# Attention with RMS-normed queries and keys, then a SwiGLU block: copies of the transposed keys on ScalarE, left sums of the output one third of a group sooner, loads of values and stores of results given out later

## The chip, the cores and the metric

The kernel runs on one core of a Trainium2 chip. The metric is the device time of one launch in microseconds (us), as the median of the runs. PE is TensorE (matrix products; PEld is its loading of weights), DVE is VectorE, ACT is ScalarE, POOL is GpSimd, and SP is SyncE, which here does nothing but issue DMAs.

## The reference

There are 8 batches of 12 heads with 448 positions of 64 elements. What is computed, in NumPy and cut to the essentials:

```python
def rmsnorm(x, g):
    return x / np.sqrt(np.mean(x * x, axis=-1, keepdims=True) + 1e-06) * g
q_n, k_n = rmsnorm(q, g_q), rmsnorm(k, g_k)
attn = softmax(q_n @ k_n.transpose(0, 1, 3, 2) / 8)
x = (attn @ v).transpose(0, 2, 1, 3).reshape(8 * 448, 768)
xn = rmsnorm(x, rms_g)
g = xn @ w_gate                                # 768 -> 1536
y = (g * sigmoid(g) * (xn @ w_val)) @ w_out    # 1536 -> 768
```

All data are float32. The rows of attention's output (3584 x 768) are the tokens of the second part.

## The kernel before

**Attention.** Each batch b has six groups of two heads, 48 groups g in all. For a group, queries and keys are loaded (`load_pair`), their squares summed (L493 on ACT, L496 on DVE), the inverse norms made on POOL (L515), keys scaled on ACT (L530) and queries on POOL (L520). `turn(g, i)` transposes: for i = 0 three transposes of queries (L544) and one of the last rows of queries and keys (L548), for i = 1 three of the keys. From the time that there is work of the second part, both use a PSUM pool of one buffer, so a transposition waits until the one before it has been copied out:

```python
    nc.scalar.activation(st["qT", g], ps[:, 0:S], ACT.Copy, scale=gqk[:, 0:1])   # L549
    nc.vector.tensor_copy(st["kT", g][:, LAST], ps[:, S:])                       # L550, 128x64
else:
    nc.vector.tensor_copy(st["kT", g][:, FULL], ps[:, FULL])                     # L552, 128x384
```

Scores (L658), exponentials on ACT (L663) and products with the values (L673) follow step by step; the sums of the exponentials are made on POOL (L708, L713, L643). The values of group g + 2 are loaded by `load_v`, two DMAs (L432) on SP, within the steps of group g.

**The second part.** When a batch's six groups are through, its tokens are normed (L725, L727, L729, L743) and their products with gate and value weights made, each as a scheme of block products with sums of the blocks on both sides: sums of the tokens (L771 on DVE), products on PE (L1177), evictions from PSUM by DVE (L1195, L1198) or ACT (L1192), and SwiGLU (L1205, L1209, L1210). The first batch's is done by plain products (L1581). The weights for it are prepared early on (integer operations, L963 on POOL, and sums of blocks, L1082 and L1085 on DVE), stored to DRAM and loaded again in blocks of 192 or 256 KB (`ask`, L1061). The sums of the blocks of output weights come from `derive_o` (L1117 on DVE), each stored by SP (L951) two steps later, and those for the second scheme of the output from `derive_q` (L1145 to L1148, stores L1152 and L1155). Side loads, of the blocks that these two need (L1043), go into places of one kind, "side". In `arena`, a memory of equal units, "side", "wg" and the others are spans of units.

**The output.** A batch's output follows while the next batch is in attention. `out_strassen` (L1442 on PE) does it with seven products of blocks. `out_quads`, used for five of the batches, nests a second scheme in each of the seven, i = 0 to 6, whose left operands are again sums (`left_q1`, L1387, three of S1 to S3 and one S4). Its products (L1513) are done in thirds, in this order on PE:

```python
for i in range(len(ORDER_Q) + 1):
    if i < len(ORDER_Q):
        steps.append((full, lambda i=i: a(i)))
    if i:
        steps.append((full // 2, lambda i=i - 1: d(i)))
    if i < len(ORDER_Q):
        steps += [(full, lambda i=i: bb(i)), (full, lambda i=i: c(i))]
```

`a`, `bb` and `c` each make two products in one PSUM bank; `d` makes one more on top of half of c's bank. On the way out DVE adds: L1533 (after ACT's copy L1532) behind a, L1538 and L1539 and the sum S4 behind bb, L1545 behind c, and then S1 to S3 of the next i; at i = 1 also those that are left of the sums of the outer scheme for the second half (`hurry(first_sums)`, L1359). L1556 follows d, then sums on POOL (L1484), and stores by SP (L1339) two steps later.

**What sets the order.** The program writes the order out by hand. `pe(fn)` advances a count of steps, gives out the instructions of fn, and then what `after(n, ...)` has put off until this step; every engine and the queue of SP work through their instructions in the order in which they were given out. Between the steps of attention, `fill` takes items of the second part from a list `todo`, as many as their share of the time allows, and after each gives out at most one sum of tokens or of left operands, and later in the group calls `derive`, `derive_o` (three times less the operations that `derive` made) and `derive_q`.

Of the kernel before, what the change touches and what calls it, by code (L numbers as in the profile page):

```python
# [12 lines left out]
ALU = mybir.AluOpType  # L13
# [322 lines left out]
def safe_scores(  # L336
# [195 lines left out]
    def turn(g, i):  # L532


        if g >= NG:
            return
        b, hp = divmod(g, NPAIR)
        if ("qT", g) not in st:
            for part in ("qT", "kT"):
                st[part, g] = qkT_pool.tile([128, S], F32, name=part)  # L540
        src = st.pop(("qn", g)) if i == 0 else st["qk", g][:, 1]
        ps = (ps_m if todo else ps_f).tile([128, 512], F32, name="tr", tag="m" if todo else "f")
        for t in range(NK):
            nc.tensor.transpose(ps[:, t * 128:(t + 1) * 128], src[:, t * 2 * D:(t + 1) * 2 * D], ident)  # L544
        if i == 0:
            if g == 0:
                warm(5)
            nc.tensor.transpose(ps[:, NK * 128:], st["rest", b][:, hp].rearrange("p h d -> p (h d)"), ident)  # L548
            nc.scalar.activation(st["qT", g], ps[:, 0:S], ACT.Copy, scale=gqk[:, 0:1])  # L549
            nc.vector.tensor_copy(st["kT", g][:, LAST], ps[:, S:])  # L550
        else:
            nc.vector.tensor_copy(st["kT", g][:, FULL], ps[:, FULL])  # L552

    def score(g, cs):

# [328 lines left out]
        after(3 if key[0:2] == ("wg", 1) else 1, free)  # L884

    def data(key):
        return st[key][0]

    def load_raw(src):
        raw = raw_pool.tile([128, 2 * BW], I32, name="raw")  # L890
# [144 lines left out]
    def ask():  # L1035

        if turn_of["n"] < TURNS:
            return
        while side and room(1, "side"):
            key = side.pop(0)  # L1040
            asked[key] = now["t"]
            st[key] = block("side")
            nc.sync.dma_start(out=data(key), in_=home(key))  # L1043
        while asked["n"] < len(uses):
            key = uses[asked["n"]]
            kind, keep_free = "wg" if key[0] == "wg" else "w", 3
            if key[1] == 1 and key[0] == "wg":
                kind, keep_free = "wg1", 6
            elif asked["derived"] < len(derived):
                return  # L1050
            if key[0] == "wo" and key[2][0] == "T" and ("kept", *key[2:]) not in asked:
                return
            if key[0] == "wq" and asked.get("sums_q", 0) < KG * (key[2] + 1):
                return
            if not room(keep_free + 1, kind):
                return
            asked["n"] += 1
            asked[key] = now["t"]
            st[key] = block(kind)
            src = home(key)  # L1060
            nc.sync.dma_start(out=data(key)[:, 0:src.shape[-1]], in_=src)  # L1061
# [68 lines left out]
    def derive_q(wait=5):  # L1130

        if not todo_q or sums_o or now["t"] - asked.get("at_q", 0) < 3 or not room(2, "wg"):
            return False
        i, j = todo_q[0]
        keys = [("wx", 2, ORDER_Q[i], c) for c in (j, j + KG)]
        for key in keys:
            if asked.get(key, now["t"]) > now["t"] - wait:
                return False
        todo_q.pop(0)
        own_a, own_b = ("ta", i, j), ("tb", i, j)  # L1140
        st[own_a], st[own_b] = block("wg"), block("wg")
        asked["at_q"] = now["t"]
        x, y, ta, tb = (data(key)[:, 0:BW].rearrange("p (h n) -> p h n", h=2) for key in (*keys, own_a, own_b))

        nc.vector.tensor_tensor(tb[:, 1], x[:, 1], x[:, 0], ALU.subtract)  # L1145
        nc.vector.tensor_tensor(ta[:, 1], y[:, 1], x[:, 1], ALU.subtract)
        nc.vector.tensor_tensor(ta[:, 0], y[:, 1], tb[:, 1], ALU.subtract)
        nc.vector.tensor_tensor(tb[:, 0], y[:, 0], ta[:, 0], ALU.subtract)  # L1148

        def store():  # L1150
            parts = kept_q[i].rearrange("p (n w) -> p n w", w=HW)
            nc.sync.dma_start(out=parts[:, j], in_=x[:, 0])  # L1152
            for src, first, second in ((y, 1, 6), (ta, 2, 3), (tb, 4, 5)):
                gap = (second - first) * KG
                nc.sync.dma_start(out=parts[:, first * KG + j:second * KG + j + 1:gap], in_=src)  # L1155
            asked["sums_q"] = asked.get("sums_q", 0) + 1

        after(1, store)
        for key in (*keys, own_a, own_b):
            after(3, lambda key=key: used(key))  # L1160
        return True
# [229 lines left out]
    def out_strassen(b):  # L1391
# [17 lines left out]
        def final(ps, pair, n, i, other=None):  # L1409
            y = y_pool.tile([128, HALF], F32, name="y", tag="y")  # L1410
            if other is None:
                nc.scalar.copy(y, ps)
            else:
                nc.vector.tensor_tensor(y, ps, add[other, pair], ALU.add)
            after(1, lambda: store(b, n, i, y))

        def done(name, pair):
            ps = bank[name, pair]
# [38 lines left out]
    def out_quads(b):  # L1457
# [19 lines left out]

        def out(what, n, first):
            for row in range(2):
                after(2, lambda row=row: store(b, n, tiles[first + row], what[row]))  # L1480

        def add(to, one, other):
            for row in range(2):
# [51 lines left out]
        def bb(i):  # L1535
# [2 lines left out]
            nc.vector.tensor_tensor(u[:, 0], ps[:, 0], st.pop(("q1", b, i)), ALU.add)  # L1538
            nc.vector.tensor_tensor(u[:, 1], ps[:, 1], u[:, 0], ALU.add)  # L1539
            left_q1(b, i, (3,))  # L1540

        def c(i):
            ps = two(i, "c")
            u3 = st["u", b, i][:, 1:2].to_broadcast([128, 2, HW])
            nc.vector.tensor_tensor(dst[i][1].rearrange("p (h n) -> p h n", h=2), ps, u3, ALU.add)  # L1545
            if i == 1:
                hurry(first_sums)
            if i + 1 < len(ORDER_Q):
                left_q1(b, i + 1, range(3))
            if i + 2 == len(ORDER_Q):  # L1550
                st["l2 done", b] = True

        def d(i):
            ps = bank[i, "c"]
# [67 lines left out]
    def fill(n=None):  # L1622

        if n is None:
            part["slot"] += 1
            upto = part["all"] * min(part["slot"] / part["slots"], 1.0)
            n = 0
            while n < len(todo) and part["spent"] + todo[n][0] / 2 < upto:
                part["spent"] += todo[n][0]
                n += 1  # L1630
        for _ in range(min(n, len(todo))):
            _, turns, sums_made, fn = todo.pop(0)
            while turn_of["n"] < turns:
                if not convert():
                    pe(idle)
            made, key = sums_made or (0, None)
            while asked["derived"] < made or (key and key not in st):
                before = dict(asked)
                derive(0)
                if key and key[0] == "wo":  # L1640
                    derive_o(0)
                ask()
                if before == asked:
                    pe(idle)
            pe(fn)
            convert()

            if first_sums:
                first_sums.pop(0)()
            elif slow and now["t"] - st["block"] > 4 and now["t"] - st["x_at"] >= NPAIR and may_make(slow[0][0]):  # L1650
                slow.pop(0)[1]()
            if 2 < now["t"] - st["block"] < 5:
                derive()
            if now["t"] - st["block"] > 4 and now["t"] != st.get("left_sums"):
                made = 0
                while made < 2:
                    done = derive()
                    if not done:
                        break
                    made += done  # L1660
                for _ in range(3 - made):
                    derive_o()
                derive_q()

# [99 lines left out]
    for g in range(NG + 1):  # L1764
# [51 lines left out]
        if g == NPAIR + 1:  # L1816
            some = lambda *parts: [exps(g, i, scores(g, i)) for i in parts]
            pe(lambda: (rests(g), some(0, 1)))
            pe(lambda: rms_x(0))
            pe(lambda: values(g - 1))  # L1820
            load_v(g + 2)
            pe(lambda: some(2, 3))
            pe(lambda: norm_x(0))
            pe(lambda: some(4, 5))
            pe(lambda: sums(g - 1))
            later_sums(g, 2)
            begin(0, 15)
        else:
            sums_due = g % 2 == 0
            pe(lambda: (totals(g - 1) if sums_due else None, step(g, 0)))  # L1830
            pe(lambda: [step(g, i) for i in (1, 2)])
            load_v(g + 2)
            pe(lambda: [step(g, i) for i in (3, 4)])
            pe(lambda: ([step(g, i) for i in (5, 6)], weigh(g - 1, 2) if sums_due else hold(g - 1)))
            if g < NG:
                later_sums(g, 2)
        st["block"] = now["t"]
        if hp:
            fill()
            norm_k(g + 1, 0)  # L1840
# [21 lines left out]
        pe(lambda: norm_x(b - 1))  # L1862
        fill()
    fill(len(todo))
    for _ in range(3):
        pe(idle)


# [36 lines left out]
```

## Time and profile before

| what | value |
|---|---|
| time, median of 3 runs | 1554.34 us (1552.52 to 1556.89) |
| time of the profiled execution | 1555.48 us |
| its span, first to last instruction | 1553.7 us |
| mean clock granted to TensorE | 0.990 |
| busy share of PE, DVE, ACT, POOL | 96%, 68%, 37%, 47% |
| DMA, mean | 208 GB/s |

The span is from the first to the last instruction of one execution, and busy times are shares of it. A row "A <- B" in the waits tells how long engine and line A stood idle until B was done; in a timeline the same stands in brackets behind the instruction, and "x3" behind an instruction is a run of three of the same kind. PEclk is the granted clock as a share of full speed. The line numbers are those of the kernel before.

### The profile page before, as it was taken

What the parts mean: (1) busy time and instruction counts of PE and PEld (TensorE: products, weight loads), DVE (VectorE), ACT (ScalarE), POOL (GpSimd) and SP (SyncE); (2) the same over time, 40 slices, a digit from 0 to 9 for tenths busy, and PEclk for the clock granted to TensorE, in tenths of its full rate; (3) what the DMA queues carried; (4) which work ended last, traced back from release to release, by engine and by line L of the source; (5) the groups of instructions that cost most, each with busy time, mean ns of one, the idle gap of its engine ahead of it and who ended that gap; (6) DMA issues with size and microseconds to landing.
All of it is one profiled execution on the core that took longest, in us unless ns stands there. A gap on an engine that the chain in (4) does not pass through costs nothing. (4 is left out here: it accounts for less than half of the span.)

```text
span 1553.7 us, 25676 instructions
## 1 busy us (share of the span) xinstructions
PE 1493.5 (96%) x8732; PEld 1163.8 (75%) x8732; DVE 1051.9 (68%) x1906; ACT 582.2 (37%) x1297; POOL 732.1 (47%) x708
## 2 busy tenths in 40 slices
PE   8999998988899999999999999999999999999997
PEld 4344444676765778888888889858788889899997
DVE  5787987688875577884668745644668745685664
ACT  6856664334322343323432253334442342201110
POOL 6867986546433353365534635435544633021002
PEclk9999999999999999999999999999999999999999
DMA  7758585666576999977456765566456664488566
GB/s 191 229 153 237 173 245 157 195 211 199 182 242 209 294 305 314 295 229 242 138 167 188 229 225 174 159 212 200 127 160 199 219 203 148 147 266 264 172 209 196
DMA packets 302176, 322.51 MB, mean 208 GB/s; under 512 B 81620, under 2 KB 243668, under 8 KB 302036
## 3 DMA queue, kind: packets, MB, share of 16 engines
q1 hardware_dynamic: 301108, 320.58, 66.5%
q8 instruction: 72, 1.18, 0.3%
q14 instruction: 68, 0.56, 0.1%
q10 hardware_dynamic: 800, 0.20, 0.1%
q0 software_dynamic: 128, 0.00, 0.0%
HBM read 266.90 MB, written 53.77 MB: 206 GB/s over the span
## 5 line engine op out<-in xcount | busy, mean ns | idle before, releaser
L1177 PE MATMUL ff<-x,w 128*128 128x224 f32 x1272 | 259.9, 359 | 0.9 <-DVE pb L1198 0.5
L713 POOL TENSOR_TENSOR es<-es,e 128x448 f32<-128x448 f32 x205 | 251.2, 1225 | 13.6
L1177 PEld LDWEIGHTS ff<-x,w 128*128 128x128 f32 x1272 | 243.5, 194 | 5.0 <-issue 1.4
L658 PE MATMUL sc<-qT,kT 64*64 64x448 f32 x1176 | 231.7, 539 | 2.3 <-DVE kT L552 2.1
L673 PE MATMUL av<-e,vt 64*64 64x448 f32 x984 | 193.2, 538 | 0.0
L663 ACT ACTIVATE e<-sc 128x448 f32<-128x448 f32 x294 | 155.3, 546 | 85.5 <-PE sc L658 69.1
L1177 PE MATMUL ff<-xs,w 128*128 128x224 f32 x848 | 168.9, 353 | 6.6 <-DMA w<-kept 4.9
L1177 PEld LDWEIGHTS ff<-xs,w 128*128 128x128 f32 x848 | 158.5, 190 | 10.8 <-issue 8.6
L643 POOL TENSOR_TENSOR ss<-ss,rd 128x448 f32<-128x448 f32 x40 | 46.7, 1169 | 209.3 <-ACT rd L642 208.0
L708 POOL TENSOR_TENSOR es<-e 128x448 f32<-128x448 f32 x41 | 47.2, 1152 | 201.9 <-ACT e L663 201.9
L658 PEld LDWEIGHTS sc<-qT,kT 64*64 64x64 f32 x1176 | 79.0, 133 | 83.3 <-issue 57.2
L1513 PE MATMUL ff<-w,l 128*128 128x192 f32 x630 | 118.6, 329 | 6.0 <-DVE l L1387 3.7
L1198 DVE TENSOR_TENSOR pc<-ff,l 128x448 f32<-128x448 f32 x56 | 34.9, 623 | 122.3 <-PE ff L1177 75.3
L515 POOL TENSOR_TENSOR rs<-ms,mhalf 128x12 f32<-128x12 f32 (+1 forms) x50 | 114.8, 2295 | 4.2
L1581 PE MATMUL ff<-x,w 128*128 128x448 f32 x288 | 114.5, 552 | 0.0
L1513 PEld LDWEIGHTS ff<-w,l 128*128 128x128 f32 x630 | 103.6, 190 | 12.1 <-DVE l L1387 5.2
L673 PEld LDWEIGHTS av<-e,vt 64*64 64x64 f32 x984 | 66.5, 133 | 41.4 <-issue 41.4
L1195 DVE TENSOR_TENSOR pb<-ff,pb 128x448 f32<-128x448 f32 x84 | 52.3, 623 | 66.2 <-PE ff L1177 58.8
L1581 PEld LDWEIGHTS ff<-x,w 128*128 128x128 f32 x288 | 54.5, 194 | 52.6 <-issue 50.6
L1177 PE MATMUL ff<-top_x,w 128*128 128x224 f32 x424 | 88.0, 357 | 2.4 <-ACT pa L1192 1.2
L1177 PEld LDWEIGHTS ff<-top_x,w 128*128 128x128 f32 x424 | 78.6, 190 | 14.2 <-issue 10.5
L1177 PE MATMUL ff<-l,w 128*128 128x224 f32 x432 | 86.8, 353 | 0.7 <-DVE pc L1198 0.7
(208 smaller groups left out, 2803.9 us busy)
## 6 DMA issues: line engine op xcount, KB each, us to landing
w<-kept SPq DMA_DIRECT2D x383, 256.0 KB, 3.7
w<-kept_q SPq DMA_DIRECT2D x350, 192.0 KB, 3.7
w<-kept_o SPq DMA_DIRECT2D x150, 192.0 KB, 3.7
kept_q<-w SPq DMA_DIRECT2D x63, 192.0 KB, 3.8
qk<-in_q_dram SPq DMA_DIRECT2D x48, 192.0 KB, 3.7
qk<-in_k_dram SPq DMA_DIRECT2D x96, 96.0 KB, 3.7
raw<-in_moe_w_gate_dram SPq DMA_DIRECT2D x24, 384.0 KB, 4.5
raw<-in_moe_w_val_dram SPq DMA_DIRECT2D x24, 384.0 KB, 3.9
```

Source lines behind the costliest of these rows:

```text
L515: nc.gpsimd.tensor_tensor(st["rs", g][:, cols], ms, mhalf[:, cols], ALU.pow)
L643: after(m, lambda: (nc.gpsimd.tensor_tensor(ss, ss, rd, ALU.add), st.update({("summed", b): hp})))
L658: nc.tensor.matmul(ps[r, 0:S], lhsT=st["kT", g][r, keys_of(i)], rhs=st["qT", g][r, :], start=True, stop=True)
L663: nc.scalar.activation(e, ps[:, 0:S], ACT.Exp)
L673: nc.tensor.matmul(st["av", g][own(j), 0:S], lhsT=vt, rhs=st["e", g, i][r], start=i == 0, stop=i == PARTS - 1, skip_group_check=True)
L708: nc.gpsimd.tensor_tensor(st["es", g], st["e", g, 0], st["e", g, 1], ALU.add)
L713: nc.gpsimd.tensor_tensor(st["es", g], st["es", g], st["e", g, i], ALU.add)
L1177: nc.tensor.matmul(bank[:, w * HT:(w + 1) * HT], lhsT=data(key)[:, (2 * w + c) * 128:(2 * w + c + 1) * 128], rhs=a[left][:, c, :], start=o ...
L1195: nc.vector.tensor_tensor(T[name], ps[:, 0:S], T[name], ALU.add)
L1198: nc.vector.tensor_tensor(T[name], ps[:, 0:S], T[other], what)
L1513: nc.tensor.matmul(ps, lhsT=a[:, j, :], rhs=data(key)[:, n % 2 * HW:(n % 2 + 1) * HW], start=start and j == 0, stop=j == KG - 1, skip_grou ...
L1581: nc.tensor.matmul(bank[w][:, 0:S], lhsT=data(key)[:, c * 128:(c + 1) * 128], rhs=st["x", 0][:, 3 * half + c, :], start=half == c == 0, st ...
```

## The change

The copies of the transposed keys are made by ScalarE in place of VectorE in those groups in which work of the second part is in the list; the first groups keep VectorE. Side loads of blocks of output weights may also take a place of the kind "wg", once more than 32 sums of gate and value weights have been derived; `data` cuts the block to its kind's width. The results' stores are given out two steps instead of one after their last operation in `out_strassen`, and four instead of two in `out_quads`. There, the left-over sums at i = 1 and S1 to S3 of the next i are given out at the end of bb(i) instead of the end of c(i), so they stand ahead of L1545 on VectorE. `derive_o` is not called in a step in which `derive` made something, and otherwise two times, three from the 33rd derived sum on. The values of group g + 2 are loaded two steps after the last of the group's own steps, not among them, and five steps instead of three without work end the program.

```diff
--- before.py
+++ after.py
@@ -539,6 +539,7 @@
             for part in ("qT", "kT"):
                 st[part, g] = qkT_pool.tile([128, S], F32, name=part)
         src = st.pop(("qn", g)) if i == 0 else st["qk", g][:, 1]
+        copy_k = nc.scalar.copy if todo else nc.vector.tensor_copy
         ps = (ps_m if todo else ps_f).tile([128, 512], F32, name="tr", tag="m" if todo else "f")
         for t in range(NK):
             nc.tensor.transpose(ps[:, t * 128:(t + 1) * 128], src[:, t * 2 * D:(t + 1) * 2 * D], ident)
@@ -547,9 +548,9 @@
                 warm(5)
             nc.tensor.transpose(ps[:, NK * 128:], st["rest", b][:, hp].rearrange("p h d -> p (h d)"), ident)
             nc.scalar.activation(st["qT", g], ps[:, 0:S], ACT.Copy, scale=gqk[:, 0:1])
-            nc.vector.tensor_copy(st["kT", g][:, LAST], ps[:, S:])
+            copy_k(st["kT", g][:, LAST], ps[:, S:])
         else:
-            nc.vector.tensor_copy(st["kT", g][:, FULL], ps[:, FULL])
+            copy_k(st["kT", g][:, FULL], ps[:, FULL])
 
     def score(g, cs):
 
@@ -884,7 +885,7 @@
         after(3 if key[0:2] == ("wg", 1) else 1, free)
 
     def data(key):
-        return st[key][0]
+        return st[key][0][:, 0:GW if key[0] == "wg" else BW]
 
     def load_raw(src):
         raw = raw_pool.tile([128, 2 * BW], I32, name="raw")
@@ -1036,10 +1037,10 @@
 
         if turn_of["n"] < TURNS:
             return
-        while side and room(1, "side"):
+        while side and (room(1, "side") or side[0][0] == "wd" and asked["derived"] > 32 and room(4, "wg")):
             key = side.pop(0)
             asked[key] = now["t"]
-            st[key] = block("side")
+            st[key] = block("side" if room(1, "side") else "wg")
             nc.sync.dma_start(out=data(key), in_=home(key))
         while asked["n"] < len(uses):
             key = uses[asked["n"]]
@@ -1140,7 +1141,7 @@
         own_a, own_b = ("ta", i, j), ("tb", i, j)
         st[own_a], st[own_b] = block("wg"), block("wg")
         asked["at_q"] = now["t"]
-        x, y, ta, tb = (data(key)[:, 0:BW].rearrange("p (h n) -> p h n", h=2) for key in (*keys, own_a, own_b))
+        x, y, ta, tb = (data(key).rearrange("p (h n) -> p h n", h=2) for key in (*keys, own_a, own_b))
 
         nc.vector.tensor_tensor(tb[:, 1], x[:, 1], x[:, 0], ALU.subtract)
         nc.vector.tensor_tensor(ta[:, 1], y[:, 1], x[:, 1], ALU.subtract)
@@ -1412,7 +1413,7 @@
                 nc.scalar.copy(y, ps)
             else:
                 nc.vector.tensor_tensor(y, ps, add[other, pair], ALU.add)
-            after(1, lambda: store(b, n, i, y))
+            after(2, lambda: store(b, n, i, y))
 
         def done(name, pair):
             ps = bank[name, pair]
@@ -1477,7 +1478,7 @@
 
         def out(what, n, first):
             for row in range(2):
-                after(2, lambda row=row: store(b, n, tiles[first + row], what[row]))
+                after(4, lambda row=row: store(b, n, tiles[first + row], what[row]))
 
         def add(to, one, other):
             for row in range(2):
@@ -1538,17 +1539,17 @@
             nc.vector.tensor_tensor(u[:, 0], ps[:, 0], st.pop(("q1", b, i)), ALU.add)
             nc.vector.tensor_tensor(u[:, 1], ps[:, 1], u[:, 0], ALU.add)
             left_q1(b, i, (3,))
-
-        def c(i):
-            ps = two(i, "c")
-            u3 = st["u", b, i][:, 1:2].to_broadcast([128, 2, HW])
-            nc.vector.tensor_tensor(dst[i][1].rearrange("p (h n) -> p h n", h=2), ps, u3, ALU.add)
             if i == 1:
                 hurry(first_sums)
             if i + 1 < len(ORDER_Q):
                 left_q1(b, i + 1, range(3))
             if i + 2 == len(ORDER_Q):
                 st["l2 done", b] = True
+
+        def c(i):
+            ps = two(i, "c")
+            u3 = st["u", b, i][:, 1:2].to_broadcast([128, 2, HW])
+            nc.vector.tensor_tensor(dst[i][1].rearrange("p (h n) -> p h n", h=2), ps, u3, ALU.add)
 
         def d(i):
             ps = bank[i, "c"]
@@ -1658,7 +1659,7 @@
                     if not done:
                         break
                     made += done
-                for _ in range(3 - made):
+                for _ in range(0 if made else 3 if asked["derived"] > 32 else 2):
                     derive_o()
                 derive_q()
 
@@ -1818,7 +1819,6 @@
             pe(lambda: (rests(g), some(0, 1)))
             pe(lambda: rms_x(0))
             pe(lambda: values(g - 1))
-            load_v(g + 2)
             pe(lambda: some(2, 3))
             pe(lambda: norm_x(0))
             pe(lambda: some(4, 5))
@@ -1829,12 +1829,12 @@
             sums_due = g % 2 == 0
             pe(lambda: (totals(g - 1) if sums_due else None, step(g, 0)))
             pe(lambda: [step(g, i) for i in (1, 2)])
-            load_v(g + 2)
             pe(lambda: [step(g, i) for i in (3, 4)])
             pe(lambda: ([step(g, i) for i in (5, 6)], weigh(g - 1, 2) if sums_due else hold(g - 1)))
             if g < NG:
                 later_sums(g, 2)
         st["block"] = now["t"]
+        after(2, lambda g=g: load_v(g + 2))
         if hp:
             fill()
             norm_k(g + 1, 0)
@@ -1862,7 +1862,7 @@
         pe(lambda: norm_x(b - 1))
         fill()
     fill(len(todo))
-    for _ in range(3):
+    for _ in range(5):
         pe(idle)
 
 
```

## Prediction

> **What bounds the kernel.** I read the page first, then the waits of PE, then a table of windows around PE's long waits, then timelines at two places. In the page the busy times are shares of the 1553.7 us span, and the slices of PEclk are tenths of full clock.
>
> ```profile
> PE 1493.5 (96%) x8732; PEld 1163.8 (75%) x8732; DVE 1051.9 (68%) x1906; ACT 582.2 (37%) x1297; POOL 732.1 (47%) x708
> PEclk9999999999999999999999999999999999999999
> ```
>
> PE carries the time. Nothing in the diff removes a matmul, so only PE's idle time (some 50 us in the trace) and stretches at a lower clock can change. The waits of PE (total, times, longest) say what ends that idle time:
>
> ```profile
> PE tr L544 <- DVE kT L550: 14.2, 5, 5.1
> PE ff L1177 <- DMA w<-kept: 4.9, 3, 3.5
> PE ff L1513 <- DVE l L1387: 3.7, 5, 1.2
> PE ff L1177 <- DVE pc L1198: 3.7, 3, 2.5
> PE sc L658 <- DVE kT L552: 2.1, 1, 2.1
> PE ff L1513 <- DVE pc L1545: 1.5, 3, 0.5
> ```
>
> The first row is the largest: the one buffer for transposes is freed only when DVE has copied the keys. Its five waits end at 240.05 (5.10 us), 428.48 (3.47), 627.51 (2.68), 814.79 (1.48) and 1163.77 (1.49), each at the boundary of two batches. Windows around two of them, and around the 3.53-us wait for weights at 510.87 (columns: length, PE, PEld, DVE, ACT, POOL busy, PEclk, DMA share, GB/s):
>
> ```profile
> 236.00:239.30 3.30, 0.00 (x0) 0.00 (x0) 3.23 (x5) 0.00 (x0) 2.96 (x3) 1.00 0.73 179
> 239.31:246.12 6.81, 6.07 (x11) 3.21 (x12) 6.60 (x16) 0.00 (x0) 4.22 (x4) 0.50 0.71 176
> 816.17:819.57 3.40, 3.40 (x11) 3.08 (x10) 1.30 (x3) 0.58 (x1) 2.80 (x3) 0.50 0.29 81
> 507.00:514.00 7.00, 3.47 (x26) 2.10 (x28) 2.19 (x6) 1.50 (x3) 0.00 (x0) 1.00 1.01 343
> ```
>
> After each of the five waits PE runs 3.4 or 6.8 us at clock 0.50; after the wait at 510.87 it does not. PE work in such a stretch takes twice its time (a matmul of L1177 every 374 ns, not 189), so half the PE busy time in it is lost: 3.04 and 2.69 us in the two long ones (at 239 and 427), 1.7 in each short one, 10.8 in all. Why DVE is late is seen at 811 to 815 (start, duration, instruction):
>
> ```profile
> 811.13 0.63 ACT L549 ACTIVATE qT<-tr,gqk 128x448 f32<-128x448 f32 x1 [5.94 <-PE tr L548]
> 811.82 1.37 DVE L1387 TENSOR_TENSOR l<-l,h 128x384 f32<-128x384 f32 x1
> 813.12 1.48 DVE L1387 TENSOR_TENSOR h<-h 128x384 f32<-128x384 f32 x1
> 814.52 0.21 DVE L550 COPY kT<-tr 128x64 f32<-128x64 f32 x1
> 814.79 0.55 PE L544 MATMUL tr<-ident,qk 128*128 128x128 f32 x3 [1.48 <-DVE kT L550]
> ```
>
> ACT was done with its half of the buffer at 811.76; the 0.21-us copy stands behind DVE's sums.
>
> **Key copies on ScalarE.** From group 8 on, 40 of 48 pairs of L550 and L552 (0.22 and 0.55 us) leave DVE: 31 us. On ACT their price is estimated from its own PSUM copies, 0.53 (L1192, 128x448) and 0.32 (L1532, 128x192): 0.48 and 0.21, 28 us on an engine 37% busy. What stands behind them there are exponentials and gate copies; the bounds are 0 and +0.7 us at each of 80 places (not below: ACT gains no time), and I take 0, since ACT is idle before most of its groups. L550's copy follows L549 at once (811.8 above), so PE no longer waits. At 240 the whole 5.10+3.04 = 8.1 goes: DVE and ACT are idle later, and the next weights lead their use by 38 us. At 627, 815, 1164: 2.68+1.7 = 4.4, 1.48+1.7 = 3.2, 1.49+1.7 = 3.2; next in line is L1195's eviction, in each case 0.5 us or more early. The single L552 wait at 188.86 adds 2.1. At 428 the 3.47+2.69 does not stand, see the next part. Sum: -21.0.
>
> Here a rule bears on it. The Trainium skill (TensorE: Matmul & The Clock Gate, Part 1: The HAM clock gate) has the clock halved only after an idle window of about 3.4 us on a free-running grid. By it the three dips after waits of 1.48 to 2.68 us would have another cause and remain (5.1 us less gained), and no new wait below 3.4 us would cause one; the sum at the end would be 1551 instead of 1547.5. The rows above, where all five waits dip, are what I sum by.
>
> **Fewer derived sums per step (L1117), side loads into a second kind of space.** Before, each late step called derive_o at least once; after, not at all where derive made something, else two or three times. In 300 to 312 DVE is always behind: four L1117 (0.55 to 0.86) stand ahead of the eviction L1198 that PE waits for (2.46 at 312.77, 0.48 at 315.04). Without them, 2.94 falls to about 0.3: 2.6. The waits at 360 to 375 (5.05) shrink by an estimated 0.9, that at 397.56 by 0.65; one at 404.96 grows by 0.5. Sum -3.65. The deferred L1117 come later: the last stands at about 438.8, the eight stores of kept_o wait for it on SP, and a load of wo behind them lands (3.7 us) at 443.0 while PE wants it at 441.15. With DVE three L1117 behind at 428 this eats the gain of that boundary; bounds -6.2 (the whole gain) to +4, taken +1.9.
>
> **Loads of values and stores later.** v loads (two DMAs, L432) are given out two steps after the group's scores instead of among them, stores two steps (out_quads) or one step (out_strassen) later. SP stands idle before L432 for 59.3 and 51.5 us (for PE) and before L1339 for 31.3 (for POOL), and loads of weights queue behind both. PE pays for late weights only in the second row of its waits, 4.9 us. At 510.87 the load goes out some 2 us sooner: 1.8 of 3.53 won (bounds 0 and 4.9; below nothing by 1.2, if the bunched kept_q stores get ahead of it). In the quads the loads of kept_q lead by 3 us or more, so deferring buys nothing there. The two more idle steps at the end issue nothing to PE: 0. Sum -1.8.
>
> **Left sums one third sooner.** In out_quads, for the batches output at 636-702, 823-890, 1172-1236, 1353-1402 and 1494-1544, PE does thirds a, (d of the one before), bb, c: two products of 0.98 us in each, one in d, 7.0 in a cycle. d(i) writes the bank that L1545 reads, and needs it 4.0 us after bb(i) ends. Before, L1545 came ahead of S1, S2, S3 (L1387) of the next i. Now they stand ahead of it. Nothing is added, only the order on DVE. Alone, the chain is .1 + .72 (L1538, L1539) + 4 x .47 + .55 (L1545), some 3.4: it fits. Two places do not. At i = 1 the three remaining hurried sums (L1359) also go ahead, back to back from 655.1 to 656.5 in the trace of before: L1545 ends 657.75 for a d at 656.36, +1.5. At i = 5 POOL contends:
>
> ```profile
> 688.73 1.29 DVE L1387 TENSOR_TENSOR l<-raw,l 128x384 f32<-128x384 f32 x1
> 689.55 5.48 POOL L713 TENSOR_TENSOR es<-es,e 128x448 f32<-128x448 f32 x4
> 691.00 0.55 DVE L1545 TENSOR_TENSOR pa<-ff,th 128x384 f32<-128x384 f32 x1
> 693.97 1.48 DVE L1387 TENSOR_TENSOR raw<-raw 128x384 f32<-128x384 f32 x1
> 694.11 1.24 PE L1513 MATMUL ff<-w,l 128*128 128x192 f32 x6 [0.76 <-DVE l L1387]
> ```
>
> The sums take 1.18 to 1.48 beside L713. From 690.0 three of them (4.0) and two L496 (1.0) put the end of L1545 at 695.6, for a d at 692.2: +3.4, less the waits of 0.92 that S1 to S3 cost PE before: +2.5. At i = 2, by the same reckoning, +1.25 if POOL stays beside it, 0 if not; i = 3 gives back 0.4. I take +0.4 for the two. That is 4.4 in each of the first three batches; the fourth, where 1.3 of waits go, +1.5; the last +1.2. Sum +15.9 (bounds: 19.4 with all contended rows, and -5.2 if nothing is late and the waits for L1387 and L1545 go). One of the three new waits of 3.4 us is taken to dip the clock (as five of nine waits above 1.4 us did), +1.7.
>
> **Sum.** -21.0 - 3.65 - 1.8 + 1.9 + 15.9 + 1.7 = -6.9. The profiled execution took 1555.48 us (span and 1.8 around it), 1.1 above the median of the runs: 1548.5 there, 1547.5 as a median. What a measurement of this kernel can tell from no change is 0.3%, 4.7 us.
>
> **Rivals.**
> - *The sums never make L1545 late except at i = 1.* For it: uncontended sums are .55, and the mean of L1387 over its groups is .62 to .86, so most stand clear of POOL; DVE also loses the 31 us of copies. Against it: POOL's L713 follows the same steps as before. Then i = 5 and i = 2 cost nothing and their waits go: 15.9 + 1.7 becomes about 2, and the time is 1532 (1529 to 1541).
> - *Slower: L1545 behind the left sums brings the clock dips back.* Every new wait above 1.2 us in the quads (three in each of three batches, two and one in the others: 12) halves the clock for 3.4 us, at 1.7 each: 20.4, and with the contended 19.4 the loss is 39.8 against 24.6 won elsewhere: +15, 1569 (1559 to 1573). It decides from six dips on with contended sums, or eight with mine. For it: a wait of 1.48 was enough at 815. Against it: those five stood beside the eight one-column matmuls of L725, and 3.53 us at 510.87 did not dip.
> - *The waits only change their name.* At the boundaries PE meets the next late item (L1195, L727, weights) as at 428, and the total stays within 4.7 us. Against it: DVE has idle time after 240 and 815.
>
> **How the numbers follow.** My sum, own range 1543 to 1553: 0.45, of which 0.11 lies within 4.7 us of before. First rival 0.20, slower rival 0.30, renamed waits 0.05. Faster .34 + .20 = 0.54, same .11 + .05 = 0.16, slower 0.30. The range leaves out a tenth at each end: half of the first rival below 1533, a third of the slower one above 1566.
>
> **What would show it.** Right: no row of L544 waiting for a key copy, clock 1.00 after 240, 627, 815 and 1164, no wait of L1177 for L1198 above 0.5; rows of L1513 waiting for L1545's line of together 15 to 22 us, longest 3 to 4, at i = 1 and i = 5. Wrong: L1513's waits below 8 us (first rival), or windows of clock 0.50 inside the quads (slower rival), or L1442 waiting over 4 us for kept_o near 441 (the deferred sums), or ACT named as the releaser of PE at the boundaries.

## The result: 0.7% slower

The changed kernel took 1564.89 us (median of 6 runs, 1563.31 to 1568.73) against 1554.01 for the kernel before (6 runs). The ratio is 1.0072, with a 95% interval of 1.0054 to 1.0090. Forecast was 1547.5, faster; the time lies inside the stated range (1533 to 1566), on the other side of the kernel before. The profiled execution, the fastest of the six, has a span of 1561.5 us, 7.8 more than before.

The page of the changed kernel has PE, DVE and ACT as follows:

```profile
PE 1491.8 (96%) x8732; PEld 1160.1 (74%) x8732; DVE 1027.2 (66%) x1826; ACT 603.8 (39%) x1377; POOL 734.1 (47%) x708
```

Eighty copies have gone from DVE to ACT: 24.7 us less on DVE, 21.6 more on ACT (the copies alone took 27.1 there; forecast 31 and 28). The busy time of PE is 1.7 us less, so the loss is idle time. In the waits of PE (line numbers are one higher than before from L545 on, and L1545 is now L1552) the names have changed:

```profile
PE ff L1514 <- DVE pa L1552: 11.2, 4, 3.3
PE ff L1514 <- DVE y L1552: 8.7, 7, 2.3
PE sc L659 <- DVE x L744: 5.5, 1, 5.5
PE ff L1178 <- DMA w<-kept: 5.4, 2, 4.2
PE ff L1514 <- DVE pb L1552: 4.5, 3, 1.5
PE ff L1178 <- DVE pb L1196: 3.6, 3, 3.0
PE ff L1178 <- DVE w L1086: 2.8, 1, 2.8
PE sc L659 <- ACT rd L699: 1.5, 1, 1.5
```

The first row of before, 14.2 us for the keys' copy, is gone. The waits for the eviction behind the left sums are now 24.4 us together (three rows), and there is a new wait for L744, where before there was none. Below, the quads are the five stretches in which `out_quads` runs, and a dip is a stretch at a granted clock of 0.50.

Since the order on PE is the same in both programs, the start of the same matmul can be compared in the two traces. The table has, at some times of the trace before, by how much the changed kernel is ahead (-) or behind (+), and the same for three kernels of the experiments:

| us in the trace before | 200 | 270 | 412 | 444 | 608 | 640 | 709 | 826 | 895 | 1090 | 1173 | 1240 | last matmul |
|---|---|---|---|---|---|---|---|---|---|---|---|---|---|
| changed | -2.2 | -1.3 | -3.1 | -2.8 | -0.1 | -4.2 | 1.3 | -2.1 | 3.1 | 1.9 | -1.6 | 5.5 | 9.1 |
| u_sums | -3.8 | -3.8 | -3.8 | -1.9 | 3.1 | -1.0 | -2.7 | -6.0 | -6.5 | -7.8 | -11.3 | -11.7 | -11.7 |
| k_only | -3.9 | -3.5 | -4.4 | -5.5 | -3.2 | -0.1 | 0.2 | -3.1 | -3.6 | -4.9 | -8.4 | -8.8 | -8.8 |
| x744 | -4.1 | -10.9 | -10.8 | -10.4 | -5.9 | -9.9 | -11.7 | -15.0 | -15.5 | -16.8 | -20.2 | -20.7 | -20.7 |

Up to 636 us the changed kernel and u_sums have the same program. Of their 2.5 us at 270, 1.6 come from the first 10 us, where no part of the change is at work yet (k_only and x744 have the same lead); the 3 us at 608 are what two executions of one program differ by. A third kernel that is the same up to there, late_i1 below, is at +6.3 at 608.

### The profile page after: what moved, and what is told of

Read it like the earlier page. It is cut to its first block, busy times and chain, and to the rows that moved or that the text cites. A ratio compares the mean times of both kernels' runs of the same rounds, so it can differ in the third digit from the quotient of the medians.

```text
span 1561.5 us, 25665 instructions
## 1 busy us (share of the span) xinstructions
PE 1491.8 (96%) x8732; PEld 1160.1 (74%) x8732; DVE 1027.2 (66%) x1826; ACT 603.8 (39%) x1377; POOL 734.1 (47%) x708
## 4 chain that ended last, share of the span: by engine, by line
PE 79%; DVE 14%; DMA 3%; issue 2%; SPq 1%; ACT 1%; POOL 0%; DVEq 0%; POOLq 0%; ACTq 0%
PE ff L1178 35%; PE ff L1514 12%; PE sc L659 7%; PE av L674 7%; PE ff L1443 5%; PE ff L1582 5%; PE tr L545 2%; PE ff L1316 2%; DVE l L1388 1%; PE den L692 1%; PE den L607 1%; PE sc L563 1%; PE av L590 1%; DVE w L1118 1%; DVE ms L496 1%
## 5 line engine op out<-in xcount | busy, mean ns | idle before, releaser
L714 POOL TENSOR_TENSOR es<-es,e 128x448 f32<-128x448 f32 x205 | 251.0, 1224 | 13.6
L1178 PE MATMUL ff<-x,w 128*128 128x224 f32 x1272 | 254.0, 353 | 1.4 <-DVE pb L1199 1.1
L1178 PEld LDWEIGHTS ff<-x,w 128*128 128x128 f32 x1272 | 238.6, 190 | 4.2 <-DVE pb L1199 1.4
L1196 DVE TENSOR_TENSOR pb<-ff,pb 128x448 f32<-128x448 f32 x84 | 52.3, 623 | 65.3 <-PE ff L1178 55.9
L1582 PEld LDWEIGHTS ff<-x,w 128*128 128x128 f32 x288 | 53.3, 190 | 51.0 <-issue 47.6
L1178 PEld LDWEIGHTS ff<-top_x,w 128*128 128x128 f32 x424 | 78.8, 190 | 13.9 <-issue 13.7
```

Of the source, the lines that this page charges most:

```text
L714: nc.gpsimd.tensor_tensor(st["es", g], st["es", g], st["e", g, i], ALU.add)
L1178: nc.tensor.matmul(bank[:, w * HT:(w + 1) * HT], lhsT=data(key)[:, (2 * w + c) * 128:(2 * w + c + 1) * 128], rhs=a[left][:, c, :], start=o ...
L1196: nc.vector.tensor_tensor(T[name], ps[:, 0:S], T[name], ALU.add)
L1582: nc.tensor.matmul(bank[w][:, 0:S], lhsT=data(key)[:, c * 128:(c + 1) * 128], rhs=st["x", 0][:, 3 * half + c, :], start=half == c == 0, st ...
```

## Experiments

**1. The left sums behind the eviction again (u_sums).** All else is as changed.

```diff
 def bb(i): ...
-    if i == 1: hurry(first_sums)
-    if i + 1 < len(ORDER_Q): left_q1(b, i + 1, range(3))
 def c(i): ...   # ends with the eviction
+    if i == 1: hurry(first_sums)
+    if i + 1 < len(ORDER_Q): left_q1(b, i + 1, range(3))
```

> The changed kernel with the left sums back behind L1545's eviction (all else changed). Theory 1: the order of these sums is the whole loss. The trace of the changed kernel has 24.4 us of waits of PE for that eviction and two clock dips of 3.4 us (1.7 us each) inside the quads, the kernel before had 5.2 us of waits there: about 20.9 us less, 1544 us (1541 to 1547), under the kernel before. Rival: VectorE is late in the quads anyway and the sums are waited for by name of L1388 instead: 1555 us or more.

Measured: 1541.94 us, ratio to before 0.9905 (0.9884 to 0.9927), as expected. Of the waits of PE for DVE in the quads this row is left, with 0.5 us more for other sums of L1388 and 0.7 for L1546:

```profile
PE ff L1514 <- DVE l L1388: 3.7, 5, 1.2
```

So the order of the sums costs 23.0 us by the medians, and 24.0 by the table from 640 us on (13.3 lost against 10.7 won); the rest of the change wins 0.95%. The rival falls.

**2. The key copies on VectorE again (u_keys).** `copy_k = nc.vector.tensor_copy`.

> The changed kernel with all key copies back on VectorE. Theory 1: the waits at the boundaries near 627, 815 and 1164 us come back with their dips (4.4 + 3.2 + 3.2) and the one near 189 us (2.1), while at 240 us the copies on ScalarE gained only some 1 us; with the copies in VectorE's way some tenths more in each late eviction: 1577 us (1573 to 1581). Rival: where the copy was waited for, VectorE is behind for good, and the wait only changes its name as it did at 240 us: 1565 us (1561 to 1569).

Measured: 1577.96 us, ratio 1.0145 (1.0127 to 1.0162): the copies are worth 13.1 us in the changed kernel. Its waits have the old row beside the new ones:

```profile
PE tr L545 <- DVE kT L551: 13.8, 5, 5.1
PE ff L1514 <- DVE pa L1552: 11.6, 4, 3.4
```

The first row's waits are 13.8 us, and dips came at three of the five (near 238, 428 and 823 us, not at 631 and 1177). That the copies are worth less than their waits and dips is what the expectation said: at 240 us the wait is handed on to L744, and at 428 the changed kernel waits as long for L1196 (3.02 us) as this one does for the copy (3.01).

**3. The old count of derived sums and side loads (u_derive).**

```diff
-for _ in range(0 if made else 3 if asked["derived"] > 32 else 2):
+for _ in range(3 - made):
...
-while side and (room(1, "side") or side[0][0] == "wd" and asked["derived"] > 32 and room(4, "wg")):
+while side and room(1, "side"):
```

> The changed kernel with the old count of derive_o and side loads into their own kind of place alone. Theory 1: the stage from 300 to 412 us loses again the 1.7 us that the change won there, and the weights' wait near 507 us (4.2 us and a dip) stays or shrinks by up to 3: 1564 us (1560 to 1567). Rival: the put-off sums cost the 8 us that the prediction missed between 412 and 607: 1558 us or less.

Measured: 1567.22 us, ratio 1.0069 (1.0044 to 1.0095), some 2 us above the changed kernel and hardly to be told from it. By stages, compared with the kernel before, it gains 0.2 us from 444 to 608, where the changed kernel loses 2.7 and u_sums 5.0; from 608 to 640 it loses 2.1, where those two win 4.1. There, in its timeline, the derived sums L1146 to L1149 still stand ahead of an eviction, and the first of them waits for a store:

```profile
625.18 0.36 DVE L1146 TENSOR_TENSOR w<-w 128x192 f32<-128x192 f32 x1 [1.74 <-DMA kept_q<-w]
626.58 0.61 DVE L1196 TENSOR_TENSOR pb<-ff,pb 128x448 f32<-128x448 f32 x1
627.24 3.35 PE L1178 MATMUL ff<-raw,w 128*128 128x224 f32 x8 [3.44 <-DVE pb L1196]
```

Fewer sums together with the second place for side loads are a trade here: later weights in one batch for a free boundary in the next. The run takes both back at once and doesn't tell them apart. The loss of 1.7 us from 300 to 412 that the expectation names did not come: u_derive wins 0.9 there, as k_only below does.

**4. Loads of values and stores as early as before (u_loads).** `load_v(g + 2)` among the group's steps, stores one and two steps after their operation.

> The changed kernel with the loads of values and the stores of results given out as early as before (three idle steps at the end). Theory 1: nothing on PE hangs on them outside 500 to 607 us: 1565 us (1562 to 1568), and no wait of PE for a DMA is longer than 4.2. Rival: they keep weight loads waiting, and the early order makes the wait near 507 us longer by 3 us or more: 1568 to 1573 us.

Measured: 1568.81 us, ratio 1.0088 (1.0072 to 1.0105), 3.9 above the changed kernel. The time lies in the rival's range, but the longest wait for a DMA is 5.3 us, 1.1 more than the changed kernel's 4.2 and not 3 more. Up to 608 us it is at +2.2, no worse than u_sums with +3.1, and in the quads one of its dips (885.6 us) lasts 6.8 us, not 3.4. The mean granted clock of its four runs is 0.986 to 0.988, that of the changed kernel's six 0.988 to 0.990; the mean difference, 0.0018, is an estimated 3 of the 3.9 us. Whether deferring is worth more than a microsecond or two is not settled, and neither is which of the loads and the stores would be.

**5. Which places pay for the sums: late_i1 and late_125.** The sums stand behind the eviction at i = 1 alone, or at i = 1, 2 and 5; elsewhere ahead of it, as changed.

```diff
 def bb(i): ...
+    if not (i in (1, 2, 5)): left_of_next(i)    # late_i1: i == 1
 def c(i): ...
+    if i in (1, 2, 5): left_of_next(i)
```

> The changed kernel, with the hurried sums and S1 to S3 of the next i given out behind L1545's eviction at i = 1 alone. Theory 1: each of five batches loses at i = 1 what the sums that go ahead last there, whatever POOL does: by the jumps in the trace of the changed kernel 1.65 us in three batches, 0.8 and 1.2 in the last two, 7 together: 1558 us (1555 to 1561). Rival: the wait moves to i = 2, since VectorE is then as far behind: 1563 us or more.

> The changed kernel, with the sums given out behind the eviction at i = 1, 2 and 5, and ahead of it at i = 0, 3 and 4. Theory 1: where no hurried sums and no work of POOL lie beside them, the sums fit ahead of the eviction and cost nothing; only the wait of 1.3 us at i = 0 in the batch near 1368 us remains: 1543.5 us (1541 to 1547), as with all sums behind. Rival: each place costs its share, and half of the 20.9 us stays: 1550 us or more.

Measured: late_i1 1567.10 (1563.25 to 1569.88), nine above the expectation and not below the changed kernel; late_125 1547.47, ratio 0.9949 (0.9935 to 0.9964), four above it. In the trace of late_i1 the waits of 1.4 us at i = 1 are gone, and those at i = 2 are 1.94 instead of 1.50 us; its profiled execution, the slowest of the six, was 6.4 us behind the changed kernel's at 608 us, in program that is the same, and in the quads it has four dips, two of them 6.8 us long, where the changed kernel has two of 3.4. The clock is lower in all six runs: 0.984 to 0.986, against 0.988 to 0.990; the mean difference, 0.0037 of 1565 us, is an estimated 5.7 us. So 0.44 us of the wait moves on to i = 2, the rival's way, and most of the rest was lost to the clock; why it dips more often here is open. late_125 has a wait that none of the others has, three times 1.76 us (the eviction is L1556 there):

```profile
667.35 1.35 DVE L1388 TENSOR_TENSOR l<-h,h 128x384 f32<-128x384 f32 x1
668.73 1.23 DVE L1388 TENSOR_TENSOR l<-l,h 128x384 f32<-128x384 f32 x1
670.89 0.55 DVE L1556 TENSOR_TENSOR pc<-ff,th 128x384 f32<-128x384 f32 x1
671.49 2.22 PE L1514 MATMUL ff<-w,l 128*128 128x192 f32 x12 [1.76 <-DVE pc L1556]
```

The wait is at i = 3, which I had counted as free of POOL. Without the waits of 1.4 and 1.5 us at i = 1 and 2, PE and VectorE get there sooner against POOL: the sums start at 667.35 us, in the changed kernel at 667.57, and POOL's additions L1485, which ran from 665.29 to 667.24 there, run from 666.97 to 669.55 here and lie beside two of the three sums. So the free places are not a property of i: they move with the rest. Both expectations that went by a list of places were too low.

**6. POOL's work taken away (no_pool).** From group 18 on, four of the five additions L714 of a group are left out, and with them the exponentials of four of seven tiles from the sums.

```diff
-after(n + 2, lambda: more(3, 4))
-after(n + 3, lambda: more(5, 6))
+if g < 18:
+    after(n + 2, lambda: more(3, 4))
+    after(n + 3, lambda: more(5, 6))
```

> The changed kernel without four of the five additions L714 of POOL per group from group 18 on (sums of exponentials of four of seven tiles are left out of the result). Theory 1: the sums of VectorE are long at i = 2 and i = 5 because POOL works beside them: L1388 falls to 0.55 us there, the waits of PE for L1552 at i = 5 (3.3 us) and i = 2 (1.5 us) go or fall under 0.5, those at i = 1 (1.4 us) stay; span 1548 us (1543 to 1553) against 1561.5. Rival: order on VectorE alone makes them, and all waits stay at their size.

Measured: a span of 1549.9 us, one execution, as expected. The same place of the quads, i = 5 in the first batch, in the timeline of the changed kernel:

```profile
688.16 5.65 POOL L714 TENSOR_TENSOR es<-es,e 128x448 f32<-128x448 f32 x4
688.54 1.48 DVE L1388 TENSOR_TENSOR l<-raw 128x384 f32<-128x384 f32 x1
690.05 1.37 DVE L1388 TENSOR_TENSOR l<-l,raw 128x384 f32<-128x384 f32 x1
691.35 1.48 DVE L1388 TENSOR_TENSOR raw<-raw 128x384 f32<-128x384 f32 x1
692.75 1.00 DVE L496 TENSOR_REDUCE ms<-sq 128x6 f32<-128x384 f32 x2
693.67 0.54 DVE L1552 TENSOR_TENSOR pa<-ff,th 128x384 f32<-128x384 f32 x1
694.26 3.15 PE L1514 MATMUL ff<-w,l 128*128 128x192 f32 x9 [3.30 <-DVE pa L1552]
```

and of the kernel without the additions (line numbers one higher):

```profile
690.54 0.55 DVE L1389 TENSOR_TENSOR l<-raw 128x384 f32<-128x384 f32 x1
691.12 0.56 DVE L1389 TENSOR_TENSOR l<-l,raw 128x384 f32<-128x384 f32 x1
691.60 0.55 DVE L1389 TENSOR_TENSOR raw<-raw 128x384 f32<-128x384 f32 x1
692.99 0.55 DVE L1553 TENSOR_TENSOR pa<-ff,th 128x384 f32<-128x384 f32 x1
693.59 2.22 PE L1515 MATMUL ff<-w,l 128*128 128x192 f32 x12 [0.63 <-DVE pa L1553]
```

The three sums take 1.66 us instead of 4.33, and the wait at i = 5 is 0.63 instead of 3.30; at i = 2 it is gone. At i = 1 it stays, 1.40 us, with its seven sums back to back and no POOL beside them. The contention is shown.

**7. The scalings of the tokens together (x744).** The kernel u_sums, and in the second batch the six L744 are given out in one step, not one in each of six steps between conversions of weights.

```diff
-            if b:
+            if b > 1:
                 after(hp, lambda hp=hp: scale(hp))
```

> The changed kernel with the left sums back behind the eviction (measured 1541.9 us) and, in the second batch, the six scalings L744 of the tokens given out together, not one per step behind the conversions of weights. Theory 1: the gain of 8.1 us at 240 us was lost because VectorE, with conversions of weights to do, frees late the bank that the scaling reads; with the scalings ahead, the wait of 5.5 us and its clock dip of 1.7 us go: 1535 us (1531 to 1538). Rival: VectorE has too much work in this stage, the conversions come later by as much as the scalings come sooner, and the wait moves to weights or evictions within some 20 us: 1540 us or more.

Measured: 1536.37 us, ratio 0.9877 (0.9846 to 0.9908), the best of the study together with the last. What the copies had won at 240 us and lost is seen in the changed kernel's timeline of DVE and PE:

```profile
250.09 1.26 DVE L744 SCALAR_TENSOR_TENSOR x<-x,rg,rb 128x448 f32<-128x448 f32 x2
253.13 0.68 DVE L744 SCALAR_TENSOR_TENSOR x<-x,rg,rb 128x448 f32<-128x448 f32 x1
255.59 0.68 DVE L744 SCALAR_TENSOR_TENSOR x<-x,rg,rb 128x448 f32<-128x448 f32 x1
257.15 0.36 DVE L914 TENSOR_SCALAR top_x<-top_x 128x384 int32<-128x384 int32 x1
258.02 1.26 DVE L744 SCALAR_TENSOR_TENSOR x<-x,rg,rb 128x448 f32<-128x448 f32 x2
259.44 1.01 PE L659 MATMUL sc<-qT,kT 64*64 64x448 f32 x2 [5.49 <-DVE x L744]
```

Between two scalings stand conversions (L913 to L915), and the last scaling frees the bank that the scores need. With the scalings together they are one row, and the wait is gone (x744):

```profile
248.19 3.63 DVE L744 SCALAR_TENSOR_TENSOR x<-x,rg,rb 128x448 f32<-128x448 f32 x6
```

The table has the gain where it belongs: -10.9 at 270 us, against -3.8 for u_sums. These 7 us are kept up to 412, so the conversions that now come later delay nothing up to there. By the medians x744 is 5.6 us under u_sums; its profiled execution is the fastest of its four runs.

**8. The copies alone, and one step more (k_only, q_store3).** k_only is the kernel before with the copies on ACT and no other part. q_store3 is x744 with `after(3, store)` for `after(1, store)` in `derive_q`, and the places free one step later.

> The kernel before with the copies of the keys on ScalarE and nothing else of the change. Theory 1: the copies carry most of what the change wins (at 189, 627, 815 and 1164 us), and the put-off sums and DMAs a few us besides: the kernel with everything but the left sums took 1541.9 us, without the loads and stores it lost 3.9 and without the put-off sums 2.3 beside the left sums: 1548 us (1544 to 1551). Rival: those two parts only traded waits inside the batch in which VectorE and the queue of SP are behind, and buy nothing: 1542 us or less.

> The kernel with the scalings L744 together (1536.4 us), and in it the stores L1153 and L1156 of the derived blocks given out three steps after their sums, not one (their places come free one step later too). Theory 1: on the queue of SP four of these stores, 1.9 us, stand right ahead of the load that PE waits for at 499.8 us (4.35 us and a clock dip of 1.7 us): that wait falls to 2.5 us or less: 1533.5 us (1530 to 1536). Rival: the load waits for its place or for the memory's bandwidth, not for its turn: 1536 us or more, with the wait at 4 us.

Measured: k_only 1546.31 us, ratio 0.9926 (0.9906 to 0.9946), as expected: the copies are most of the gain. At the boundary from 608 to 640 us it loses 3.1, however. There the longest wait of this row, with a dip of 6.8 us after 630, takes the place of the wait for the keys' copy:

```profile
PE ff L1178 <- DVE pb L1196: 7.7, 3, 4.3
```

q_store3 took 1535.58 us (1532.49 to 1541.13), not to be told from x744. The load that PE waits for lands 2.05 us sooner, but PE gets there 1.7 sooner too, and the wait is 4.0 us after 4.35, the size that the rival names; what sets the moment of this load is open.

## Why the prediction was wrong

The sum was -6.9, the spans of the two profiled executions differ by +7.8 (the medians by +10.9). By the stages of the table:

- *Key copies, -21.0.* At 189 us -2.2 (forecast -2.1), at the boundary of 608 to 640 -4.1 (-4.4), at 815 -3.4 (-3.2), at 1164 -3.5 (-3.2). The failed step is the 8.1 us at 240. I wrote "DVE and ACT are idle later" and looked at the trace of before, where DVE has pauses of 2.44 and 1.16 us after 246:

```profile
248.71 0.62 DVE L1590 SCALAR_TENSOR_TENSOR h<-th,ff 128x448 f32<-128x448 f32 x1 [2.44 <-ACT th L1589]
252.64 0.62 DVE L1592 SCALAR_TENSOR_TENSOR h<-h,ff 128x448 f32<-128x448 f32 x1 [1.16 <-PE ff L1581]
261.77 1.26 DVE L743 SCALAR_TENSOR_TENSOR x<-x,rg,rb 128x448 f32<-128x448 f32 x2
```

These pauses were there because PE had stood still for 5.1 us and run at half clock after it, while DVE worked off its queue. The 8.1 us did come: PE is 9.2 us ahead at 250 us, after 1.0 at 230. But the last scaling (L743, now L744) ends only 3.75 us sooner than before (259.28 us against 263.03), and PE waits 5.49 us for it, some 20 us after the old wait, and dips. From 200 to 270 us 0.9 is lost in all: 8.2 won at 240, 7.9 lost again by 270, and 1.2 lost at 215 us, where PE, 2.2 us ahead, waits for ACT's L699. The step at 240 is 9.0 of the 14.7 us between sum and result; x744 shows that most of it could have been had.
- *Fewer derived sums, -3.65 and +1.9.* From 300 to 412 us 1.7 came, with single executions of the same program between 0 and 1.7, so at most half of the term. The wait of 2.46 us at 312.77 went, those at 397.56 and 404.96 changed as forecast (0.96 to 0.36, 0.75 to 1.30); the wrong part is the stretch of 360 to 375, where the wait for L1086 grew from 1.13 to 2.77 us. With the old count k_only and u_derive have it at 1.1 and win 0.9 in the stage, so no gain of fewer sums is shown there. The loss at 428 was 0.3, in u_sums 1.9. It came in part as forecast, by an eviction (3.0 us for L1196) that stood behind L1118, and in u_sums by a wait of 2.45 us for a load of kept_o at 437.
- *Loads, -1.8.* From 444 to 608 us 2.7 were lost in the profiled execution, 5.0 to 6.0 in u_sums, late_i1 and late_125, the same program up to there. The wait for weights is 4.2 us, where 1.7 was forecast. With the old count of derived sums and the old places of side loads 0.2 was won (u_derive), and 2.3 lost with the old loads as well (k_only, which has a dip there). So deferring the loads may have won what I put down to it, by one pair of executions; what I had wrong is the other part of the change, fewer derived sums per step with a second place for side loads, whose cost near 507 us I had only as a bound (+1.2, for bunched stores). How it makes the weights late there is not shown: giving those stores out later (q_store3) left the wait at 4.0 us.
- *Left sums, +15.9 and +1.7 for a dip.* The step was right in its places, and in its sizes but for i = 2: at i = 1 1.40 us (forecast 1.5), at i = 5 3.30 (3.4), with POOL as the cause of the second. At i = 2 and 3 I took +0.4 of bounds of +0.85 and -0.4, and the wait at i = 2 was 1.50, with POOL beside it. With two dips, not one, and 3.6 us, not 2.7, in the last two batches, the quads lost 21.4 us (forecast 17.6).

The slower rival had the time (1559 to 1573) but not the mechanism. It needed six dips and contended sums; the sums were contended at i = 2 and 5 as it says, the dips two of the twelve. It came out near the time because the 24.6 us that it counts as won elsewhere did not all come. Of the first rival nothing is left: the sums were late at three of the six places in each of three batches.

The clock: "five of nine waits above 1.4 us" was no rate that could be carried over. In the changed kernel's quads three waits of 3.30 us dipped twice, and eight of 1.40 to 2.27 never; in u_keys one of 2.27 us did (1390.5 us). Dips are part of the steps above: after the first 20 us half clock cost PE 9.0 us (half its busy time in the dips at 257, 431, 506, 694 and 1233 us), where the sum left 4.4 of the 10.8 before. The Trainium skill (TensorE: Matmul & The Clock Gate, Part 1: The HAM clock gate), by which only an idle window of some 3.4 us halves the clock, is nearer to these than to the waits of 1.48 and 1.49 us before. It does not fit them all: in late_i1 a wait of 1.94 us at 668 us was followed by a dip at 669.5. The sum by that reading, 1551, was 13.9 us off, mine 17.4; but the three dips near 627, 815 and 1164 us that it would have kept went with their waits.

## What to carry to other kernels

Idle time of an engine behind a stall is no slack: if the stall goes, the consumer moves up, so lay the producers' work against the moved times over the whole next stage before counting a gain. An eviction that a matmul waits for should not stand behind sums that are needed later, above all where another engine's work beside them can stretch each sum from 0.55 to 1.48 us. And a bundle should be taken apart: here one move cost 23 us and hid a gain of 12.

## What the runs showed of the hardware

- Equal waits do not all dip. Of the three waits of 3.30 us in the changed kernel, those before 694.4 and 1233.7 us were followed by 3.4 us at half clock, and the one in between, ending at 883.77, was not:

```profile
694.40:697.80 3.40, 3.40 (x11) 3.40 (x12) 2.03 (x5) 0.00 (x0) 3.32 (x3) 0.50 0.21 68
883.80:887.20 3.40, 3.40 (x21) 3.40 (x22) 2.33 (x6) 0.00 (x0) 3.32 (x3) 1.00 0.46 104
```

In these two windows (length, busy PE, PEld, DVE, ACT, POOL, then PEclk) PE is busy throughout, with half the matmuls in the first. Between executions of the same program it differs too: at 370 us u_sums has a dip of 3.4 us after the wait of 2.77 us for L1086, and the changed kernel has none.

- VectorE's additions of two operands in SBUF can stretch beside POOL's additions. In the changed kernel the sums L1388 with no work of POOL beside them took 0.54 to 0.56 us. Of 27 beside POOL's L714, 24 took 1.16 to 1.50; of 21 beside POOL's L1485, 14 still took 0.55 or 0.56 and three 1.15 to 1.38. VectorE's evictions from PSUM did not stretch (0.54 to 0.56 for L1552, alone and beside L714 or L1485), nor did L496 (0.53 to 0.55). What makes the difference among the sums is open.
